# A gated mix of a state-space convolution and a squared-ReLU layer, backward pass: the S4 loop written out as a software pipeline, and FFT intermediates on other DMA queues

## The chip, the cores and the metric

The kernel runs on one core of a Trainium2 chip. The core has a matrix engine (TensorE, PE), a vector engine (VectorE, DVE), a scalar engine (ScalarE, ACT), a general engine (GpSimd, POOL) and SyncE (SP), which issues transfers; ACT and POOL issue transfers as well. Each engine works through its own queue of instructions in the order in which it was written. The metric is the device time of one execution in microseconds (us).

## The reference

The reference computes a mix of two branches and the gradients of all inputs. Cut to what matters:

```python
def A(u, A_re, A_im, B_re, B_im, C_re, C_im, log_dt, Dskip):   # S4 branch, D=448, N=256, L=2048
    dt = exp(log_dt)[:, None]
    logdA = dt * (A_re + 1j * A_im)
    P = exp(logdA[:, :, None] * arange(L))
    K = einsum("dn,dnl,dn->dl", C, P, dt * B).real
    return causal_conv_by_fft(u, K) + u * Dskip
def B(x, w1, b1, w2, b2):                                       # F=1792
    return relu(x @ w1 + b1) ** 2 @ w2 + b2
def f(u, ..., gate_w):
    g = sigmoid((u * gate_w).sum(-1, keepdims=True))
    return g * A(u, ...) + (1 - g) * B(u, ...)
out, vjp = jax.vjp(f, ...)
return out, *vjp(grad_out)
```

## The kernel before, in words

The S4 branch needs, for each of the 448 channels, the sequence K of 2048 values (a sum over 256 modes of powers of a complex number) and, backward, the sums of dK against the same powers. A power with exponent l is split into two factors, of 32 and of 64 steps, so that two small tables stand for it.

**S4 loop (lines 557 to 679).** It goes over NCH = 14 chunks of 32 channels (4 groups g of 8). For each chunk `build` makes table X (in the tile XW) in 4 doublings and table Y in 5, each doubling three operations on DVE (L549 and L550 multiply, L555 adds) with n = 4 to 32 for X and n = 2 to 32 for Y; ACT writes the first entries (L567 to L580). `kgen` multiplies the tables into K's values (128 matmuls at L593, out by one ACT cast, L597). `tables_t` transposes X on PE (L613) and copies it out on ACT (L614). `load_yt` transposes one group of Y by a DMA from SP (L622). `back` multiplies the transposed Y with dK (PE, L642; the second half of its weights is a scaled copy of dK by ACT, L631), casts the result (ACT, L645), forms two products per group on DVE (L654, 8 for a chunk), and sums these on PE (L663) into one PSUM tile kept over two chunks. X, Y and the PSUM tile for `kgen` and the transposes have one buffer each; the transposed Y (YT) and the products have three, the cast result two.

dK comes from an FFT correlation of `grad_out` and u ahead of the loop: `fwd1` (L173, evacuated alternately on ACT at L159 and DVE at L161), written to memory (gd, L178), read back (`load_s1`, L182), `fwd2` (L192), complex products (L202 to L207), `inv1` (L220), written and read back again (hd, L224 and L229), in four quarters q. After the loop K goes the same way.

**What sets the order.** A framework takes the program text in the order written, schedules it by its own costs, and writes each engine's queue; waits between engines are semaphores. Work of the dense branch fills in: its forward pass (L502, L513) lies beside the correlation, its backward pass beside the S4 loop, as loads by DMA transposes (L774, L810; weights at L786, L802) and matmuls (stage 1 at L779, stage 2 at L821). `K.dma()` gives its transfers to SP and ACT by turns.

In the loop one chunk follows the other:

```python
    for c in range(NCH):
        build(c)
        kgen(c)
        XTs = tables_t(c)
        back(c, XTs, [load_yt(g) for g in range(3)])
```

## Time and profile before

| what | value |
|---|---|
| time, median of 3 runs | 1341.72 us (1338.66 to 1354.12) |
| profiled execution, its own time | 1360.1 us |
| span of that execution in the trace | 1358.3 us |
| PE busy | 726.1 us (53%) |
| DVE busy | 865.4 us (64%) |
| ACT busy | 558.4 us (41%) |
| POOL busy | 136.7 us (10%) |
| mean granted clock of PE | 0.716 |

No engine is busy throughout. The page cuts the span into 40 slices; DVE's busy share by slice is `3465788666094673280857759659568573199994` in tenths, and the share of the 16 DMA engines `9988664758977979969576640440431429754886`. Read together with the lines that run, the stretches are: loads (0 to 60 us), `fwd1` of u and `grad_out` (60 to 100), the dense forward pass (100 to 240), the rest of the correlation and the first table build (240 to 328), the S4 loop with the dense backward pass beside its first part (328 to 1139), K's FFT (1139 to 1200), and the end (1200 to 1358). A row of a timeline gives start, duration, engine, line, operation and tiles, and in brackets the idle time of the engine just before and what ended it.

### The profile page before, as it was taken

Reading aid. Unit: us, or ns where it says so; the run is one execution under the profiler, and the core shown is the slowest. Engines: PE = TensorE matmul, PEld = TensorE weight load, DVE = VectorE, ACT = ScalarE, POOL = GpSimd, SP = SyncE. Lnnn points to the kernel's source line nnn. Section 1 sums busy time; section 2 is a strip of 40 time slices with the busy share of each in tenths; the row PEclk is TensorE's granted clock in tenths of the full one; section 3 lists DMA queues with packets and bytes.
Section 4 is the critical chain, followed back from the end, with each engine's and each line's share of the span. In section 5 each row is a group of like instructions: output and inputs, shape, how many; then the busy total and the mean of one; then the engine's idle time right before and its main releaser. Section 6 shows DMA issues by size and latency. Waiting matters only on the chain. (4 is left out here: it accounts for less than half of the span.)

```text
span 1358.3 us, 17800 instructions
## 1 busy us (share of the span) xinstructions
PE 726.1 (53%) x7088; PEld 323.8 (24%) x7088; DVE 865.4 (64%) x1102; ACT 558.4 (41%) x865; POOL 136.7 (10%) x244
## 2 busy tenths in 40 slices
PE   0456999432297793466987541431513405334467
PEld 0111222111144352223443221221312303111112
DVE  3465788666094673280857759659568573199994
ACT  1256998443265352322563442533423503323302
POOL 1001331000011211121212001001001001000000
PEclk9976999765598997677998655656555656555559
DMA  9988664758977979969576640440431429754886
GB/s 201 210 182 287 214 212 178 263 173 192 185 142 161 199 160 147 145 111 122 158 176 157 127 70 21 76 67 21 79 53 34 67 20 231 221 160 153 243 187 133
DMA packets 300012, 201.74 MB, mean 149 GB/s; under 512 B 235685, under 2 KB 281769, under 8 KB 299033
## 3 DMA queue, kind: packets, MB, share of 16 engines
q1 hardware_dynamic: 252280, 96.03, 37.4%
q0 software_dynamic: 17952, 65.85, 16.5%
q10 hardware_dynamic: 29696, 38.72, 11.3%
q8 instruction: 55, 0.90, 0.3%
q14 instruction: 29, 0.23, 0.1%
HBM read 78.23 MB, written 67.44 MB: 107 GB/s over the span
## 5 line engine op out<-in xcount | busy, mean ns | idle before, releaser
L654 DVE TENSOR_TENSOR P<-R 128x2048 bf16<-128x2048 bf16 x112 | 133.9, 1223 | 307.4 <-ACT R L645 296.2
L645 ACT CAST R<-psF 128x1024 bf16<-128x1024 f32 x112 | 115.2, 1051 | 43.1 <-PE psF L642 34.2
L593 PE MATMUL psX<-Y,X 128*32 128x64 bf16 x1792 | 24.8, 223 | 200.0 <-DVE Y L555 198.2
L642 PE MATMUL psF<-R,K 64*32 64x256 bf16 x896 | 56.2, 396 | 133.2 <-DMA R<-Y 91.0
L159 ACT CAST st<-psF 128x896 bf16<-128x896 f32 x69 | 60.8, 909 | 111.2 <-PE psF L220 56.1
L663 PE MATMUL psS<-P,cb_sel 128*32 128x256 bf16 x896 | 91.2, 321 | 19.5 <-DVE P L654 19.3
L614 ACT COPY R<-psX 128x1024 bf16<-128x1024 bf16 x56 | 56.9, 1015 | 58.3 <-PE psX L613 58.2
L555 DVE TENSOR_TENSOR Y<-Y,F 128x256 bf16<-128x256 bf16 (+4 forms) x70 | 70.5, 1007 | 2.4
L593 PEld LDWEIGHTS <-X 128*32 128x32 bf16 x1792 | 22.9, 113 | 204.8 <-DVE Y L555 162.1
L549 DVE TENSOR_TENSOR Y<-Y,F 128x256 bf16<-128x256 bf16 (+4 forms) x70 | 70.4, 1006 | 1.9
L550 DVE TENSOR_TENSOR F<-Y,F 128x256 bf16<-128x256 bf16 (+4 forms) x70 | 69.7, 995 | 0.4
L549 DVE TENSOR_TENSOR X<-X,F 128x512 bf16<-128x512 bf16 (+3 forms) x56 | 64.8, 1158 | 1.9 <-ACT F L567 0.5
L550 DVE TENSOR_TENSOR F<-X,F 128x512 bf16<-128x512 bf16 (+3 forms) x56 | 64.5, 1151 | 1.9 <-ACT F L568 1.9
L555 DVE TENSOR_TENSOR X<-X,F 128x512 bf16<-128x512 bf16 (+3 forms) x56 | 64.8, 1156 | 1.4
L663 PEld LDWEIGHTS <-cb_sel 128*32 128x32 bf16 x896 | 52.4, 109 | 54.4 <-issue 45.0
L642 PEld LDWEIGHTS <-K 64*32 64x32 bf16 x896 | 24.9, 155 | 157.6 <-issue 64.6
L161 DVE CAST st<-psF 128x896 bf16<-128x896 f32 x27 | 29.4, 1089 | 51.0 <-DMA gd<-st 26.4
L821 PE MATMUL psN<-D,S 128*128 128x448 bf16 x224 | 51.3, 377 | 16.5 <-DMA S<-dhT_d 16.5
L821 PEld LDWEIGHTS <-S 128*128 128x128 bf16 x448 | 42.5, 102 | 70.0 <-DMA S<-dhT_d 18.7
L613 PE MATMUL psX<-ident,X 128*128 128x128 bf16 x448 | 52.7, 291 | 11.7 <-ACT R L614 10.7
L220 PE MATMUL psF<-P,cb_MI 64*128 64x448 bf16 x128 | 28.8, 560 | 56.1 <-DVE P L204 25.1
L642 PE MATMUL psF<-R,S 64*32 64x256 bf16 x896 | 57.5, 365 | 0.5 <-ACT S L631 0.5
(202 smaller groups left out, 1520.8 us busy)
## 6 DMA issues: line engine op xcount, KB each, us to landing
hT_d<-R POOLq DMA_DIRECT2D x14, 512.0 KB, 3.8
sp<-K POOLq DMA_DIRECT2D x8, 896.0 KB, 5.1
dhT_d<-R POOLq DMA_DIRECT2D x14, 512.0 KB, 3.6
S<-hT_d POOLq DMA_DIRECT2D x8, 896.0 KB, 8.0
S<-dhT_d POOLq DMA_DIRECT2D x8, 896.0 KB, 6.8
rec_d<-rec POOLq DMA_DIRECT2D x14, 416.0 KB, 4.0
rec<-rec_d POOLq DMA_DIRECT2D x14, 416.0 KB, 3.5
gd<-st ACTq DMA_DIRECT2D x24, 224.0 KB, 3.7
```

The costliest lines, as they stand in the source:

```text
L159: nc.scalar.copy(dst, src)
L549: V.tensor_tensor(out=hi, in0=lo, in1=bcast_dims(pr, [0, (None, n // 2), 1]), op=ALU.mult)
L550: V.tensor_tensor(out=Vv.rearrange("p (x a q) -> p x a q", x=rows, q=2), in0=lo, in1=bcast_dims(pi, [0, (None, n // 2), 1]), op=ALU.mult)
L555: V.tensor_tensor(out=T4[:, :, :, n:2 * n], in0=T4[:, :, :, n:2 * n], in1=V4, op=ALU.add)
L593: T_.matmul(ps[32 * g:32 * g + 32, i * 64:(i + 1) * 64], lhsT=XW[:, 1 - t, w, :, 1], rhs=Y[:, w, t, :], start=(k == 0), stop=(k == 3), til ...
L613: T_.transpose(pt[:, 2 * t + i2, h * P:(h + 1) * P], XW[:, t, w:w + 4, :, 0].rearrange("p w a -> p (w a)"), ident[:])
L614: S.copy(XT[:, gg].rearrange("p t i n -> p (t i n)"), pt[:].rearrange("p a n -> p (a n)"))
L642: T_.matmul(psz[32 * ii:32 * ii + 32, t, 256 * s:256 * s + 256], lhsT=(DK[64 * t:64 * t + 64, :, d] if s == 0 else DKB[64 * t:64 * t + 64, ...
L645: S.copy(zb[:, :, :, i2, :], psz[:].rearrange("p t (s n) -> p t s n", s=2))
L654: V.tensor_tensor(out=pr.rearrange("p t s i n -> p t s (i n)"), in0=zv, in1=(xb if r == 0 else rev_dim(xb, 1)), op=ALU.mult)
L663: T_.matmul(sps[32 * gr:32 * gr + 32, r, :], lhsT=sel[:, k, off:off + 32], rhs=Q[r][:, t, s, i2, :], start=(g < 2 and cc == 0 and i2 == 0 ...
L821: T_.matmul(ps[:, 0:D], lhsT=blk[w][:, j, P * tt:P * tt + P], rhs=(w2n if w == 0 else w1T)[:, j, :], start=(w == 1 and j == 0), stop=(j == ...
```

## The change

Two things change. First, the transfers of FFT intermediates: all gd and hd writes go to ACT's queue (they went to SP and ACT by turns), all reads of them to SP's, and the write of the spectra (L454) goes from POOL's queue to ACT's. The turns that other loads take with `K.dma()` shift with it. Second, `build` is split into `build_x` and `build_y`, `tables_t` into its two pairs of groups, `back` into two halves, and the loop is written so that the tables of chunk c are built among the products of chunk c−1. The number of buffers does not change. Behind the loop every line number is higher than before by 3 to 13: L593 is now L596, L597 L600, L614 L616, L622 L624, L642 L645, L645 L648, L654 L657, L663 L666, L774 L787, L802 L815, L821 L834.

```diff
@@ fwd1, load_s1
-                    self.dma().dma_start(dst, st[g2 * 64:(g2 + 1) * 64])
+                    nc.scalar.dma_start(dst, st[g2 * 64:(g2 + 1) * 64])
...
-        self.dma().dma_start(s1.rearrange("p a d -> p (a d)"), src)
+        self.nc.sync.dma_start(s1.rearrange("p a d -> p (a d)"), src)
@@ inv1, load_hs
-            self.dma().dma_start(dst, st[:])
+            nc.scalar.dma_start(dst, st[:])
...
-            self.dma().dma_start(hs[64 * hp:64 * hp + 64].rearrange("p g x d -> p g (x d)"), src)
+            self.nc.sync.dma_start(hs[64 * hp:64 * hp + 64].rearrange("p g x d -> p g (x d)"), src)
@@ spectra
-            nc.gpsimd.dma_start(dst, sp.rearrange("p a r d -> p (a r d)"))
+            nc.scalar.dma_start(dst, sp.rearrange("p a r d -> p (a r d)"))
@@ the loop
-    for c in range(NCH):
-        build(c)
-        kgen(c)
-        XTs = tables_t(c)
-        back(c, XTs, [load_yt(g) for g in range(3)])
+    XTs, YTs = {}, {}
+    for c in range(NCH + 1):
+        if c < NCH:
+            build_x(c)
+            XTs[c] = tables_t(c, 0)
+        if c > 0:
+            back(c - 1, XTs[c - 1], YTs[c - 1], 0)
+        if c < NCH:
+            XTs[c] += tables_t(c, 1)
+            build_y(c)
+            kgen(c)
+        if c > 0:
+            back(c - 1, XTs[c - 1], YTs[c - 1], 1)
+        if c < NCH:
+            YTs[c] = [load_yt(g) for g in range(3)]
```

How the queues stand, at three places. DVE, the end of one chunk's table build and the start of the next chunk's, before (X and Y are the tables, R holds the cast results and transposed tables, P the products, F scratch):

```order
L549 TENSOR_TENSOR Y_271_1934<-Y_271_1934,F_273_1936 128x128x32
L550 TENSOR_TENSOR F_273_1936<-Y_271_1934,F_273_1936 128x4096
L555 TENSOR_TENSOR Y_271_1934<-Y_271_1934,F_273_1936 128x128x32
L654 TENSOR_TENSOR P_276_1939<-R_275_1938 128x2048 x7
L549 TENSOR_TENSOR X_272_1935<-X_272_1935,F_273_1936 128x128x4
L654 TENSOR_TENSOR P_276_1939<-R_275_1938 128x2048
L550 TENSOR_TENSOR F_273_1936<-X_272_1935,F_273_1936 128x512
```

DVE in the change, the same place, from the start of a chunk's build of X:

```order
L549 TENSOR_TENSOR X_272_1935<-X_272_1935,F_273_1936 128x128x4
L550 TENSOR_TENSOR F_273_1936<-X_272_1935,F_273_1936 128x512
L555 TENSOR_TENSOR X_272_1935<-X_272_1935,F_273_1936 128x128x4
L549 TENSOR_TENSOR X_272_1935<-X_272_1935,F_273_1936 128x128x8
L550 TENSOR_TENSOR F_273_1936<-X_272_1935,F_273_1936 128x1024
L657 TENSOR_TENSOR P_276_1939<-R_275_1938 128x2048
L555 TENSOR_TENSOR X_272_1935<-X_272_1935,F_273_1936 128x128x8
L657 TENSOR_TENSOR P_276_1939<-R_275_1938 128x2048
L549 TENSOR_TENSOR X_272_1935<-X_272_1935,F_273_1936 128x128x16
L550 TENSOR_TENSOR F_273_1936<-X_272_1935,F_273_1936 128x2048
L657 TENSOR_TENSOR P_276_1939<-R_275_1938 128x2048
L555 TENSOR_TENSOR X_272_1935<-X_272_1935,F_273_1936 128x128x16
```

Before, the eight products of a chunk stand behind both its tables, seven of them together. Now products of the chunk before (L657) stand one by one inside the doublings, from X's n = 8 on; a chunk's last eight operations of Y (n = 8 and above) have none between them.

ACT, from the cast of K's values on, before:

```order
L597 CAST st_6075<-psX_5946 128x512
L569 COPY X_272_1935<-rec_6349 128x128
L572 COPY X_272_1935<-rec_6349 128x128
L614 COPY R_275_1938<-psX_6078 128x1024
L645 CAST R_275_1938<-psF_6122 128x4x256
L614 COPY R_275_1938<-psX_6088 128x1024
L645 CAST R_275_1938<-psF_6140 128x4x256
L614 COPY R_275_1938<-psX_6098 128x1024
```

ACT in the change, from the same cast on (L672 is the copy of the sums, once in two chunks):

```order
L600 CAST st_6442<-psX_6313 128x512
L672 COPY st_6553<-psS_5727 128x512
L570 COPY X_272_1935<-rec_6566 128x128
L573 COPY X_272_1935<-rec_6566 128x128
L648 CAST R_275_1938<-psF_6610 128x4x256
L648 CAST R_275_1938<-psF_6628 128x4x256
L648 CAST R_275_1938<-psF_6665 128x4x256
```

The copies that seed the next table X (L569 and L572 before, L570 and L573 now) stand directly behind the cast in both. Before, copies of transposed tables (L614) alternate with the casts of `back` (L645); now four casts (L648) follow each other, and the copies of tables (L616) stand later.

SP, the transposes of the loop's second chunk among loads of the dense backward pass (L774 and L787 for stage 1), before:

```order
L774 DMA_TRANSPOSE S_274_1937<-hT_d 128x16x128
L622 DMA_TRANSPOSE R_275_1938<-Y_271_1934 128x16x128 x3
L786 DMA_TRANSPOSE S_274_1937<-S_274_1937 128x4x128
L622 DMA_TRANSPOSE R_275_1938<-Y_271_1934 128x16x128
L774 DMA_TRANSPOSE S_274_1937<-dhT_d 128x16x128
```

SP in the change, the transposes of the first and the second chunk:

```order
L624 DMA_TRANSPOSE R_275_1938<-Y_271_1934 128x16x128 x2
L799 DMA_TRANSPOSE S_274_1937<-S_274_1937 128x4x128
L787 DMA_TRANSPOSE S_274_1937<-hT_d 128x16x128
L624 DMA_TRANSPOSE R_275_1938<-Y_271_1934 128x16x128
L787 DMA_TRANSPOSE S_274_1937<-dhT_d 128x16x128 x3
L624 DMA_TRANSPOSE R_275_1938<-Y_271_1934 128x16x128 x4
L799 DMA_TRANSPOSE S_274_1937<-S_274_1937 128x4x128
```

Before, one chunk's four transposes of Y stood three and one with a weight load between; eleven loads stood ahead of the second chunk's. Now five loads in all stand between the first chunk's third transpose and the second chunk's first, and the second chunk's four stand together.

## Rows read from the trace of the kernel before

**Rows 1.** Windows: length, busy PE, PEld, DVE, ACT, POOL (count), PEclk, DMA share, GB/s.

```profile
100.00:240.00 140.00, 126.09 (x476) 35.04 (x475) 105.44 (x172) 116.73 (x249) 33.74 (x57) 0.91 0.66 225
328.40:608.00 279.60, 174.01 (x1937) 91.19 (x1937) 149.04 (x140) 109.20 (x172) 38.61 (x62) 0.77 0.90 158
608.00:793.20 185.20, 129.36 (x1457) 66.55 (x1455) 113.05 (x106) 77.69 (x112) 27.11 (x39) 0.84 0.66 137
793.20:1113.90 320.70, 110.03 (x2112) 69.44 (x2112) 225.03 (x210) 119.58 (x157) 17.83 (x35) 0.56 0.30 52
```

**Rows 2.** Timeline, ACT: the cast of K's values, chunks 0, 1, 8 and 13.

```profile
330.42 0.58 ACT L597 CAST st<-psX 128x512 bf16<-128x512 f32 x1 [2.99 <-PE psX L593]
411.81 0.59 ACT L597 CAST st<-psX 128x512 bf16<-128x512 f32 x1 [2.65 <-PE psX L593]
849.16 0.58 ACT L597 CAST st<-psX 128x512 bf16<-128x512 f32 x1 [3.01 <-PE psX L593]
1115.94 0.59 ACT L597 CAST st<-psX 128x512 bf16<-128x512 f32 x1 [33.00 <-PE psX L593]
```

**Rows 3.** Timeline, all engines, around the start of chunk 7's products.

```profile
790.89 2.29 DVE L555 TENSOR_TENSOR Y<-Y,F 128x4096 bf16<-128x4096 bf16 x1
793.33 1.93 PE L593 MATMUL psX<-Y,X 128*32 128x64 bf16 x128 [21.95 <-DVE Y L555]
796.08 1.07 ACT L572 COPY X<-rec 128x128 bf16<-128x128 bf16 x1
799.04 0.48 PE L642 MATMUL psF<-R,K 64*32 64x256 bf16 x8 [3.78 <-DMA R<-Y]
801.63 1.02 ACT L645 CAST R<-psF 128x1024 bf16<-128x1024 f32 x1
804.80 2.36 DVE L654 TENSOR_TENSOR P<-R 128x2048 bf16<-128x2048 bf16 x2 [11.62 <-ACT R L645]
817.36 0.42 DVE L549 TENSOR_TENSOR X<-X,F 128x512 bf16<-128x512 bf16 x1
```

**Rows 4.** Page, costliest groups: the products.

```profile
L654 DVE TENSOR_TENSOR P<-R 128x2048 bf16<-128x2048 bf16 x112 | 133.9, 1223 | 307.4 <-ACT R L645 296.2
```

**Rows 5.** Lines by shape, DVE, 793.2 to 1113.9 us (six chunks).

```profile
L654 DVE TENSOR_TENSOR P<-R 128x2048 bf16<-128x2048 bf16 x48 | 57.7, 1223 | 92.3 <-ACT R L645 88.9 <-PE psS L663 3.3
L549 DVE TENSOR_TENSOR X<-X,F 128x1024 bf16<-128x1024 bf16 x6 | 4.2, 693 | 0.2
```

**Rows 6.** Timeline, SP, DVE and PE, around chunk 3's products.

```profile
522.84 28.67 SPq L802 DMA_TRANSPOSE D<-in_B_w_dram  x2
551.61 9.01 SPq L622 DMA_TRANSPOSE R<-Y  x3
562.02 2.36 DVE L654 TENSOR_TENSOR P<-R 128x2048 bf16<-128x2048 bf16 x2 [41.73 <-ACT R L645]
608.62 13.80 SPq L622 DMA_TRANSPOSE R<-Y  x3
626.77 4.73 PE L821 MATMUL psN<-D,S 128*128 128x448 bf16 x14 [7.53 <-DMA S<-dhT_d]
633.72 1.40 PE L593 MATMUL psX<-Y,X 128*32 128x64 bf16 x128
```

**Rows 7.** Timeline, PE: the first matmuls of the first chunk's products.

```profile
362.53 0.69 PE L642 MATMUL psF<-R,K 64*32 64x256 bf16 x16 [30.43 <-DMA K<-dk_d]
```

**Rows 8.** Timeline, PE: `inv1` of two successive quarters of the correlation.

```profile
249.92 0.93 PE L220 MATMUL psF<-D,cb_MI 64*128 64x448 bf16 x4 [5.24 <-DVE D L204]
267.63 0.93 PE L220 MATMUL psF<-D,cb_MI 64*128 64x448 bf16 x4 [4.25 <-DVE D L204]
```

**Rows 9.** Windows: one quarter of the correlation; columns as in rows 1.

```profile
249.92:267.63 17.71, 8.71 (x48) 3.31 (x49) 10.73 (x11) 7.05 (x8) 1.06 (x2) 0.69 0.74 277
```

**Rows 10.** Line L178 (gd writes): issue time (least, median, greatest ns), and who waited (us, times).

```profile
L178 ACTq DMA_DIRECT2D gd<-st x24: 582/608/760, 31.1 to 1172.3; - x24
  ACT st L159: 26.7, 12
```

More of the change, by code (lines that the diff above doesn't have):

```diff
@@ L559, with build_x @@
     xi = yi = zi = pi_ = ki = 0
-    sps = None
-    def build(c):
+    sps = rec = None
+    def build_x(c):
+        nonlocal rec
         rec = K.t("rec", [P, NF, W2])
@@ L598, in kgen, with tables_t @@
         G_.dma_start(bass.AP(tensor=k_d, offset=c * P * 512, ap=[[512, P], [1, 512]]), kst[:])
-    def tables_t(c):
+    def tables_t(c, gp):
         nonlocal xi
         XTs = []
-        for gp in range(2):
-            XT = RB[:, xi % 3].rearrange("p (g t i n) -> p g t i n", g=2, t=2, i=2)
-            xi += 1
-            for gg in range(2):
-                g = 2 * gp + gg
-                pt = K.ps("X", [P, 4, 256], bf16)
-                for t in range(2):
-                    for i2 in range(2):
-                        for h in range(2):
-                            w = g * 16 + h * 8 + 4 * i2
-                            T_.transpose(pt[:, 2 * t + i2, h * P:(h + 1) * P], XW[:, t, w:w + 4, :, 0].rearrange("p w a -> p (w a)"), ident[:])
-                S.copy(XT[:, gg].rearrange("p t i n -> p (t i n)"), pt[:].rearrange("p a n -> p (a n)"))
-                XTs.append(XT[:, gg])
+        XT = RB[:, xi % 3].rearrange("p (g t i n) -> p g t i n", g=2, t=2, i=2)
+        xi += 1
+        for gg in range(2):
+            g = 2 * gp + gg
+            pt = K.ps("X", [P, 4, 256], bf16)
+            for t in range(2):
+                for i2 in range(2):
+                    for h in range(2):
+                        w = g * 16 + h * 8 + 4 * i2
+                        T_.transpose(pt[:, 2 * t + i2, h * P:(h + 1) * P], XW[:, t, w:w + 4, :, 0].rearrange("p w a -> p (w a)"), ident[:])
+            S.copy(XT[:, gg].rearrange("p t i n -> p (t i n)"), pt[:].rearrange("p a n -> p (a n)"))
+            XTs.append(XT[:, gg])
         return XTs
@@ L623, in load_yt, with back @@
         return YT
-    def back(c, XTs, YTs):
+    def back(c, XTs, YTs, half):
         nonlocal zi, pi_, sps
         cc = c % GC
-        if cc == 0:
+        if cc == 0 and half == 0:
             sps = K.ps("S", [P, 2, 256])
         DKB = DKBs[:, c % 2]
-        S.activation(DKB, DK[:].rearrange("p a (g x) -> p a g x", g=NG)[:, :, :, CW * c:CW * (c + 1)], ACT.Copy, scale=brow[:, 0:1])
-        for g in range(NG):
+        if half == 0:
+            S.activation(DKB, DK[:].rearrange("p a (g x) -> p a g x", g=NG)[:, :, :, CW * c:CW * (c + 1)], ACT.Copy, scale=brow[:, 0:1])
+        for g in (2 * half, 2 * half + 1):
             zb = RB[:, 6 + zi % 2].rearrange("p (t s i n) -> p t s i n", t=2, s=2, i=2)
@@ L665, in back @@
                                       tile_position=(0, 32 * gr), skip_group_check=True)
-        if cc == GC - 1:
+        if cc == GC - 1 and half == 1:
             gi = c // GC
```

1 line of the change is left out of this document (added).

## The prediction, made before the change was run

> **What bounds the kernel now.** I read the windows by stretch first [rows 1]: the reader is to see in each which engine is busy nearly throughout. From 100 to 240 us it is PE (126.09 of 140). In the first part of the S4 loop (328.4 to 608) no engine is, but the transfer engines are at 0.90. From 608 to 793.2 nothing is (DVE 113.05 of 185.2, transfers 0.66). In six chunks without dense work beside them (793.2 to 1113.9, clean chunks below) DVE has 225.03 of 320.7 us, 37.5 for a chunk, and transfers are at 0.30.
>
> Next the cast of K's values, which comes once in a chunk, as a clock [rows 2]: chunk 0 to 1 takes 81.4 us, chunk 0 to 8 518.7, chunk 8 to 13 266.8, which is 53.4 for a clean chunk against DVE's 37.5. So 15.9 us in each is idle DVE. The timeline says where [rows 3]: table Y ends at 793.18, its transposes start, and the first product starts at 804.80 after 11.62 us, released by the cast of `back`; the next X starts at 817.36, after the products. Over the loop the products wait 307.4 us, 296.2 of them for that cast [rows 4]; in the six clean chunks 92.3, or 15.4 each [rows 5]. DVE's chain there is Y, transpose, matmul, cast, products, next X, next Y, one after another. The chain runs through a stall of DVE that other DVE work could fill.
>
> **The change, part by part.**
>
> **Clean chunks.** The work on every engine is the same; what moves is the products, out of the place behind Y into the next X and Y. After Y's end, T, the next X can't start at once: it has one buffer, which K's matmuls read, and ACT seeds it behind the cast. Those stand in the old order: matmuls at 793.33, the last seed copy from 796.08 for 1.07 [rows 3], so X starts at T + 4.0. Ahead of the first product stand three operations of 0.42 (n = 4, rows 3) and two of 0.69 (n = 8, [rows 5]), 2.65 together, to T + 6.65. The first product needs a transposed Y, landed at T + 5.9 (799.04 against 793.18), 16 matmuls, about 1.0 as two of the groups of 8 take 0.48 each, and two casts of 1.02 [rows 3]: T + 8.9. DVE waits 2.3 there. Later casts have doublings of DVE between them; I count 0.5 for small gaps, and 0.7 for the copy of the sums every second chunk and the sums that products wait for (3.3 in six chunks, rows 5). The chunk is 4.0 + 2.3 + 0.5 + 0.7 + 37.5 = 45.0. The ends: 44.3 without the 0.7; 47.0 if the first product still starts 11.62 after T (idle 11.62 − 2.65 = 9.0, plus 0.5). I take 45.0, since the copies of X's tables that stood between the first casts now stand behind them. Five intervals (8 to 13): 266.8 − 225 = **−42** (−45 to −32). The last chunk's products have no table build to lie in, as before: 0.
>
> **Chunks beside dense work.** Here transfers set the pace. Their work from 328.4 to 793.2 is 0.90 × 279.6 + 0.66 × 185.2 = 374 us at full share [rows 1]. A clean chunk's own is 0.30 × 320.7 / 6 = 16.0, seven chunks 112; 262 is left for the dense work and dK. Chunk 0 to 8 then needs 262 + 8 × 16 = 390. At the 0.90 that the first part shows this is 433 us; at the mean share of both, 374 / 464.8 = 0.80, it is 487. Eight chunks of 45 are 360, so DVE isn't the limit. The two ends are rows of the same stretch; the new order spreads the loads more evenly over the chunks than the old (11 ahead of the second chunk's transposes, now 5), but keeps the weight loads ahead of a chunk's transposes: at 522.84 they hold SP for 28.67 us, Y's transposes start at 551.61, and DVE has idled 41.73 when its product starts at 562.02 [rows 6]. That stall is met one chunk later in the new order, so it stays. I take the middle, 460: **−59** (−86 to −32). The first chunk's wait for dK, 30.43 on PE [rows 7], lies in this sum: only X's first two doublings and a bit of the second chunk can be done before it.
>
> **The queues.** In the new order one more quarter of the correlation is inverted inside the dense forward pass. A quarter takes 17.71 us from one to the next [rows 8], 8.71 of it PE work [rows 9]; PE is what bounds the stretch it moves into, so 17.7 − 8.7 = −9. Against that, both halves of each gd write are now issued by ACT, one behind the other, 0.608 each [rows 10], ahead of ACT's next evacuation. The evacuation waits for these writes already (26.7 us in 12 times). Sixteen tiles ahead of the loop and eight behind it: 9.7 and 4.9 if all is on the path, 0 if the second buffer hides it; I take half, +5 and +2. The eight spectra writes moved from POOL to ACT, some 5 us of issue at the same price, lie beside PE in a stretch with ACT at 116.73 of 140 [rows 1]: 0, or +5 without that cover. Of the 24 hd writes half come over to ACT, 7 us at that price, each behind its own evacuation: 0, or +7 if all delay the next. Sum −4 and +2; the ends are −9 (no issue on the path) and +27 (all of them, and the quarter gains nothing).
>
> By the Trainium skill, page "DMA: Bandwidth & Descriptors", section "Issuing engines are not separate DMA queues", the issuing engine changes nothing but sequencer time, all transfers running on the same 16 engines. If so the −9 would be 0 and the total 9 us higher; the trace here shows no run with the other queues, and SP's 28.67-us weight load ahead of Y's transposes shows that what stands behind what in one queue does cost time.
>
> **Sum.** −42 − 59 − 4 + 2 = −103. The profiled execution took 1360.1 us, 18.4 (1.4%) above the median of 1341.7; taken off the median this gives **1238** (1257 for an execution like the profiled one). This case runs from −45 − 86 − 9 = −140 (1202) to −32 − 32 + 27 = −37 (1305).
>
> **Rivals.**
>
> *Transfers don't limit (faster).* If loads find gaps, every chunk takes 45 and only dK's wait of 30 stays: 8 × 45 + 30 = 390, −129 − 42 − 2 = −173, 1169. For it: the share falls to 0.66 in the second part. Against: 0.90 in the first.
>
> *The dense stretch gives nothing.* A late transpose of Y now holds up not only products but the table build, since a product stands in the middle of it and DVE takes its queue in order; before, the build was done by then. And the dense matmuls stay ahead of K's: Y's end had long come and transposes had started (608.62) when K's matmuls ran at 633.72, behind a dense group that itself waited 7.53 for its load [rows 6]. The next X waits for K's matmuls. If this eats the gain, −42 − 2 = −44, 1298.
>
> *Slower: these stalls add up.* If all eight intervals beside dense work become as long as the first, 81.4 [rows 2], they make 651, +132; with −44 from the rest it is +88, 1430. It decides from a mean interval of (518.7 + 44) / 8 = 70.3 us on, where it was 64.8. Against it: the dense work is unchanged, its 262 us of transfers leave room in 519, and the wait for dK, which makes the first interval long, comes once.
>
> By the Trainium skill, page "TensorE: Matmul & The Clock Gate", section "Architectural detail: the array is 16× 32×32, not 1× 128×128", PE's queue pulls only weight loads forward, and ACT and DVE are strict first-in-first-out. The trace agrees: the ready matmuls of K stood behind the 7.53-us wait. This is the rule that speaks against the change, and what it would make of the time are the last two cases.
>
> *The change doesn't do what it says.* K's matmuls, X's seeds and Y's transposes all start at Y's end as before. If the wait only moves into the doublings, the clean chunk stays 53.4 and the time about 1340. Against it: work of 2.65 us and more stands between, and X is free 4.0 us after Y's end.
>
> **How the numbers follow.** The forecast has 0.62, the unlimited case 0.08, no gain beside dense work 0.18, slower 0.06, no effect 0.06. The forecast and the third case fill 1202 to 1305; with some room below for the spread of the runs the range is 1195 to 1305, which leaves out the 0.20 of the others. 1% is 13 us, about what can be told from no change: faster 0.62 + 0.08 + 0.18 = 0.88, same 0.06, slower 0.06.
>
> **What would show it.** In clean chunks the casts of K's values some 45 us apart, 4.0 us from Y's end to the next X, and a wait of 2 to 3 us, not 11.6, before a chunk's first product. Chunk 0 to 8 in about 460 us, with transfers at 0.85 or so. The first cast about 4 us earlier than 330.42. I am wrong if clean chunks stay above 48 us, which fails the main step; if DVE waits for casts inside the doublings beside dense work for more than some 10 us a chunk, which is the third case; or if the stretch from chunk 0 to 8 passes 563 us, which is the fourth.

## The result, and the profile after

The changed kernel takes 1249.14 us (median of 4 runs, 1246.45 to 1258.18), the kernel before 1344.81 (1338.66 to 1354.12): the ratio is 0.9295, with a 95% interval of 0.922 to 0.9369. It is 95.7 us faster; 103 were forecast, and 1238 us. The profiled executions stand apart by more, 113.7 us of span (1358.3 to 1244.6), since that of before was 15.3 above its median and that of after (1246.45) is 2.7 below. Which part of the kernel holds those 15.3 us isn't known.

Rows of engines and lines, from the page of the kernel after. First what answers to the table of before, then the products [rows 4] and the first operation of X's doublings (busy, mean ns | idle time before it, what ended it):

```profile
PE 719.5 (58%) x7088; PEld 315.2 (25%) x7088; DVE 855.9 (69%) x1102; ACT 559.8 (45%) x865; POOL 131.8 (11%) x236
L657 DVE TENSOR_TENSOR P<-R 128x2048 bf16<-128x2048 bf16 x112 | 136.7, 1223 | 141.7 <-ACT R L648 107.8
L549 DVE TENSOR_TENSOR X<-X,F 128x512 bf16<-128x512 bf16 (+3 forms) x56 | 64.8, 1157 | 58.1 <-ACT X L573 57.0
```

The work is the same (DVE 865.4 us before, 855.9 now); the products' idle time fell from 307.4 us to 141.7, and 58.1 us, nearly all new, stand before X's first doubling.

The cast of K's values as a clock, after (timeline of ACT; answers to [rows 2]; chunks 0, 5, 8 and 13):

```profile
340.00 0.58 ACT L600 CAST st<-psX 128x512 bf16<-128x512 f32 x1 [2.12 <-PE psX L596]
638.27 0.58 ACT L600 CAST st<-psX 128x512 bf16<-128x512 f32 x1 [2.65 <-PE psX L596]
792.82 0.58 ACT L600 CAST st<-psX 128x512 bf16<-128x512 f32 x1 [2.55 <-PE psX L596]
1008.37 0.58 ACT L600 CAST st<-psX 128x512 bf16<-128x512 f32 x1 [11.44 <-PE psX L596]
```

The table takes the time apart by this clock (of the profiled executions, so a piece of before can be too long by part of those 15.3 us). The time from one chunk's cast to the next is called an interval below.

| piece | before | after | difference | forecast |
|---|---|---|---|---|
| start to the first cast | 330.4 | 340.0 | +9.6 | −4 |
| chunk 0 to 8, beside dense work | 518.7 | 452.8 | −65.9 | −59 |
| chunk 8 to 13, clean | 266.8 | 215.5 | −51.2 | −42 |
| last cast to the end | 242.4 | 236.2 | −6.1 | +2 |
| sum of the spans | 1358.3 | 1244.6 | −113.7 | −103 |

A clean chunk takes 43.1 us, 53.4 before. Its start, after (timeline, all engines; answers to [rows 3]): the end of Y, K's matmuls, X's first operation, the first matmuls of the products, their first two casts, and the first product.

```profile
788.45 2.29 DVE L555 TENSOR_TENSOR Y<-Y,F 128x4096 bf16<-128x4096 bf16 x1
790.79 1.96 PE L596 MATMUL psX<-Y,X 128*32 128x64 bf16 x128 [7.90 <-DVE Y L555]
795.15 0.43 DVE L549 TENSOR_TENSOR X<-X,F 128x512 bf16<-128x512 bf16 x1 [4.41 <-ACT X L573]
797.12 0.47 PE L645 MATMUL psF<-R,K 64*32 64x256 bf16 x8 [4.37 <-DMA R<-Y]
797.87 1.93 ACT L648 CAST R<-psF 128x1024 bf16<-128x1024 f32 x2 [2.75 <-PE psF L645]
799.83 1.23 DVE L657 TENSOR_TENSOR P<-R 128x2048 bf16<-128x2048 bf16 x1 [2.12 <-ACT R L648]
```

Y ends at 790.74. X starts 4.4 us later (3.9 in chunks without the copy of the sums), where 4.0 were forecast. The first product starts 9.1 us after Y's end (8.2 in the next chunk), where 8.9 were forecast, after a wait of 2.12, forecast 2.3; before, the wait was 11.62. The pipeline does in the clean part what it was said to do.

Windows of the kernel after, with the columns of [rows 1], cut at casts: chunk 0, chunks 1 to 3, chunk 4, chunks 5 to 7, and the five clean chunks:

```profile
340.00:412.00 72.00, 34.78 (x390) 16.37 (x393) 37.34 (x35) 32.58 (x50) 3.64 (x7) 0.62 0.81 172
412.00:562.00 150.00, 124.83 (x1486) 64.07 (x1475) 109.98 (x105) 76.95 (x118) 24.43 (x41) 0.88 0.87 170
562.00:638.00 76.00, 39.99 (x473) 20.44 (x474) 36.61 (x35) 25.31 (x38) 16.35 (x23) 0.73 0.88 153
638.00:793.00 155.00, 114.22 (x1418) 57.99 (x1407) 110.14 (x105) 74.66 (x107) 23.81 (x35) 0.86 0.70 151
793.00:1008.00 215.00, 88.30 (x1772) 57.36 (x1774) 183.25 (x175) 98.29 (x128) 16.71 (x33) 0.61 0.38 69
```

Transfers are at 0.81 to 0.88 until chunk 5 and at 0.70 from there to chunk 8, some 0.80 over the stretch, where 0.85 or so was forecast. That share turned out not to be the reason for the pace there.

### The profile page after: what moved, and what is told of

It reads as the page before. It is cut to its first block, busy times and chain, and to the rows that moved or that the text cites. A ratio compares the mean times of both kernels' runs of the same rounds, so it can differ in the third digit from the quotient of the medians.

```text
span 1244.6 us, 17711 instructions
## 1 busy us (share of the span) xinstructions
PE 719.5 (58%) x7088; PEld 315.2 (25%) x7088; DVE 855.9 (69%) x1102; ACT 559.8 (45%) x865; POOL 131.8 (11%) x236
## 5 line engine op out<-in xcount | busy, mean ns | idle before, releaser
L657 DVE TENSOR_TENSOR P<-R 128x2048 bf16<-128x2048 bf16 x112 | 136.7, 1223 | 141.7 <-ACT R L648 107.8
L648 ACT CAST R<-psF 128x1024 bf16<-128x1024 f32 x112 | 112.4, 1047 | 107.9 <-PE psF L645 101.6
L645 PE MATMUL psF<-R,K 64*32 64x256 bf16 x896 | 53.3, 414 | 159.3 <-DMA R<-Y 129.7
L549 DVE TENSOR_TENSOR X<-X,F 128x512 bf16<-128x512 bf16 (+3 forms) x56 | 64.8, 1157 | 58.1 <-ACT X L573 57.0
L666 PE MATMUL psS<-P,cb_sel 128*32 128x256 bf16 x896 | 89.5, 321 | 4.9 <-DVE P L657 3.9
L616 ACT COPY R<-psX 128x1024 bf16<-128x1024 bf16 x56 | 58.0, 1035 | 50.8 <-PE psX L615 48.0
L645 PEld LDWEIGHTS <-K 64*32 64x32 bf16 x896 | 26.8, 154 | 191.5 <-issue 113.6
L615 PE MATMUL psX<-ident,X 128*128 128x128 bf16 x448 | 42.3, 250 | 38.3 <-DVE X L555 30.9
L596 PE MATMUL psX<-Y,X 128*32 128x64 bf16 x1792 | 24.0, 221 | 67.2 <-DVE Y L555 67.2
L666 PEld LDWEIGHTS <-cb_sel 128*32 128x32 bf16 x896 | 51.7, 109 | 42.3 <-issue 32.1
L792 PE MATMUL psN<-D,S 128*128 128x448 bf16 x224 | 55.7, 378 | 5.8 <-ACT D L775 4.8
L792 PE MATMUL psN<-U,S 128*128 128x449 bf16 x224 | 53.6, 378 | 2.6 <-DMA S<-dhT_d 2.6
L834 PE MATMUL psN<-U,S 128*128 128x448 bf16 x224 | 53.8, 376 | 0.0
```

What stands on the lines that cost most here:

```text
L549: V.tensor_tensor(out=hi, in0=lo, in1=bcast_dims(pr, [0, (None, n // 2), 1]), op=ALU.mult)
L615: T_.transpose(pt[:, 2 * t + i2, h * P:(h + 1) * P], XW[:, t, w:w + 4, :, 0].rearrange("p w a -> p (w a)"), ident[:])
L616: S.copy(XT[:, gg].rearrange("p t i n -> p (t i n)"), pt[:].rearrange("p a n -> p (a n)"))
L645: T_.matmul(psz[32 * ii:32 * ii + 32, t, 256 * s:256 * s + 256], lhsT=(DK[64 * t:64 * t + 64, :, d] if s == 0 else DKB[64 * t:64 * t + 64, ...
L648: S.copy(zb[:, :, :, i2, :], psz[:].rearrange("p t (s n) -> p t s n", s=2))
L657: V.tensor_tensor(out=pr.rearrange("p t s i n -> p t s (i n)"), in0=zv, in1=(xb if r == 0 else rev_dim(xb, 1)), op=ALU.mult)
```

## The experiments

Each kernel was run beside the kernel before; ratios are to that, and the changed kernel's own is 0.9295. The runs of before gave medians from 1344.8 to 1355.4 from set to set, so two kernels of different sets that lie within some 10 us are told apart by their profiles alone. The runs with the queue moves, the pipeline, the weight loads left out, and the products behind all of X are one set; those with the bias gradient as rows, half of the dense loads, the products behind the middle of X, and X's seeds on DVE a second; the other four a third; the changed kernel stands apart from all three. Lines are those of the changed kernel unless the kernel before is named.

### The queue moves alone

```diff
  (the kernel before, with only)
-                    self.dma().dma_start(dst, st[g2 * 64:(g2 + 1) * 64])
+                    nc.scalar.dma_start(dst, st[g2 * 64:(g2 + 1) * 64])
...
  (and the other four moves of the change; the loop as it was)
```

> The kernel before with the queue moves alone; the loop is as before. Theory A (the pipeline made the whole gain, the queue moves cost time ahead of the loop): the first cast of K's values comes at about 338 us against 330.4 before, the clean chunk stays at 53.4, and the time is 5 to 10 us above before. Theory B (the queue moves change nothing, only who issues): within 3 us of before. Theory C (part of the 95 us came from a freer SP queue beside the dense backward pass): chunk 0 to 8 falls from 518.7 to below 500 and the time is 15 us or more below before.

Measured: 1347.28 us, 0.9966 (0.9934 to 0.9998). In the profile the first cast comes at 341.9 (before: 330.4), chunk 0 to 8 takes 496.1 (518.7), a clean chunk 53.1, the rest 239.0 (242.4). Theory A is right on the start and on the clean chunks, and wrong on the sum, since 22.6 us came back beside dense work, which is the first half of theory C: the 113.4-us interval of before has no counterpart, another one of 88.7 stands a chunk earlier. In the medians it is next to nothing, as B said, so some of the 22.6 can be the 15.3 us by which the profile of before lies above its median. The first matmul that needs dK runs at 377.47, 15 us later than in the kernel before [rows 7].

### The pipeline alone

```diff
  (the changed kernel, with all five queue moves undone)
-                    nc.scalar.dma_start(dst, st[g2 * 64:(g2 + 1) * 64])
+                    self.dma().dma_start(dst, st[g2 * 64:(g2 + 1) * 64])
...
```

> The changed kernel with all queue moves undone, the pipelined loop alone. Theory A: the first cast comes at about 330 us instead of 340.0, chunk 0 to 8 takes about 453 and the clean chunk 43.1 as in the changed kernel; the time is 5 to 10 us below the changed kernel, about 1240. Theory B: the same time as the changed kernel, within 3 us. Theory C: chunk 0 to 8 is longer than 470 and the time 15 us or more above the changed kernel.

Measured: 1254.33 us, 0.9295 (0.924 to 0.9351): the same ratio as with the moves, which is theory B. So the pipeline makes the gain, and the moves add nothing that can be measured. The pieces differ, though. The timeline of DVE in this kernel, the end of the first Y and the next X:

```profile
327.11 2.29 DVE L555 TENSOR_TENSOR Y<-Y,F 128x4096 bf16<-128x4096 bf16 x1
364.04 0.43 DVE L549 TENSOR_TENSOR X<-X,F 128x512 bf16<-128x512 bf16 x1 [34.64 <-ACT X L573]
```

The first table is ready at 329.4 (after: 337.94), but the next X waits 34.64 us, because its seed copies stand on ACT behind the scaled copy of dK. The first matmul with dK runs at 360.42 instead of 373.99, and the clock reaches chunk 8 at 785.3 against 792.8. Behind the loop the old queues lose it again: 245.3 us from the last cast to the end against 236.2.

### Dense weight loads left out

```diff
-    for dt in range(DT):
-        z = DSZ[dt]
-        nc.sync.dma_start_transpose(out=w1T[:, :, dt * P:dt * P + z], in_=B_w1[dt * P:dt * P + z, :])
...
-                    T_.matmul(..., rhs=(w2n if w == 0 else w1T)[:, j, :],
+                    T_.matmul(..., rhs=w2n[:, j, :],
```

> The changed kernel without the four transposed loads of the dense branch's weights w1 that stand ahead of one chunk's transposes of Y; the last dense products use w2 in their place. Theory A (late transposes of Y, held up in SP's queue, stop the whole table build on DVE, since a product stands in its middle): the wait of 31.3 us in chunk 4 to 5 falls below 12 and that interval from 76.1 to about 53, the time by about 22 us. Theory B (the transfer engines set the pace of the stretch, whatever the order): the time falls by the loads' own share alone, under 10 us, and the wait turns up elsewhere in chunks 5 to 8. Theory C (PE's dense products ahead of K's matmuls set the pace): no change within 3 us.

Measured: 1248.79 us, 0.9254 (0.9218 to 0.929), within the noise of the changed kernel. The first product of the chunk that stalls, in this kernel (timeline, DVE):

```profile
592.77 1.23 DVE L657 TENSOR_TENSOR P<-R 128x2048 bf16<-128x2048 bf16 x1 [23.04 <-ACT R L648]
```

It still waits 23.04 us, and the interval is 69.2 instead of 76.1. Theory A is refuted in its size: 8 us of the wait go with the weight loads, which let the transposes of Y be issued 6.5 us earlier (562.29, not 568.77); the larger part stays, and the time with it, as theory B said. What is that part? The same place in the changed kernel, POOL's timeline, then two windows (columns as above), then the product:

```profile
562.56 1.09 POOL L804 DMA_DIRECT2D out_dram<-db  x1 [2.87 <-ACT db L798]
588.49 0.50 POOL L677 DMA_DIRECT2D s_d<-st  x1 [19.80 <-DMA out_dram<-db]
```
```profile
570.00:575.00 5.00, 0.00 (x0) 0.00 (x0) 0.00 (x0) 0.00 (x0) 0.00 (x0) 0.50 0.88 9
575.00:580.00 5.00, 0.00 (x0) 0.00 (x0) 0.00 (x0) 0.00 (x0) 0.00 (x0) 0.50 0.56 21
```
```profile
599.09 1.23 DVE L657 TENSOR_TENSOR P<-R 128x2048 bf16<-128x2048 bf16 x1 [31.32 <-ACT R L648]
```

At 562.56 POOL issues the gradient of the bias b1: 3.5 KB, an array of 128 partitions by 14 values whose neighbours in memory lie on different partitions, so by its access pattern it is 1792 single values of 2 bytes. POOL's next wait for it ends at 588.49. From 570 to 580 no engine computes, and the transfer engines, 0.88 and 0.56 busy, move 9 and 21 GB/s. A write of 3.5 KB is under way there, and everything behind it waits; the next run takes it away.

### The bias gradient as rows

```diff
-    G_.dma_start(out_11.rearrange("(t p) -> p t", p=P), db1[:])
+    pdb = K.ps(NT[ni % 2], [P, 4, 256], bf16)
+    ni += 1
+    T_.transpose(pdb[0:FT, 0, 0:P], db1[:], ident[:])
+    dbr = const.tile([FT, P], bf16, name="dbr")
+    S.copy(dbr[:], pdb[0:FT, 0, 0:P])
+    G_.dma_start(out_11.rearrange("(t p) -> t p", p=P), dbr[:])
```

> The changed kernel with the gradient of the bias b1 (3.5 KB, written before in pieces of 2 bytes) turned by PE first and written as 14 rows of 256 bytes; nothing else. Theory A (that write clogs the transfer engines: from 570 to 585 us they show 0.56 to 0.89 busy and move 9 to 130 GB/s while all compute engines stand still, and POOL waits 19.8 us for it): the wait of 31.3 us in chunk 4 to 5 falls below 12, the interval from 76.1 to about 53, the time by 18 to 25 us. Theory B (the large w2 load, 1568 KB and 29.4 us to landing, and the loads beside it make the stall): the wait stays above 20 and the time within 5 us.

Measured: 1233.42 us, 0.9108 (0.9048 to 0.9168), 16 us below the changed kernel, and the two intervals of the ratios don't meet. The same product, in this kernel:

```profile
583.39 1.23 DVE L657 TENSOR_TENSOR P<-R 128x2048 bf16<-128x2048 bf16 x1 [14.21 <-ACT R L648]
```

The wait falls from 31.32 to 14.21, the interval from 76.1 to 58.8. Theory A, with its size a little high. The load of w2 (1568 KB) that B named takes 29.4 us to land in the changed kernel and 12.6 here, so it was held up itself. The 14.21 us that are left lie behind it and behind the transposed loads of w1, after which Y's transposes are issued here (576.05); no run left w2 out. The edit also moves the write: it needs a transpose and a copy first and is issued at 575.70, behind the load of w2, where the old one stood ahead of it. Its shape and its place weren't tried apart.

### The bias gradient as rows, in the kernel before

The edit above, in the kernel before.

> The kernel before with the bias gradient written as 14 rows of 256 bytes. Theory A: there the write (at 573.4 us) comes after DVE's 41.73-us wait (to 562.0), which is the w1 loads', but it clogs the loads of the dense second stage after it, and K's matmuls at 633.7 stand behind the matmuls that wait for these; interval 3 to 4 falls from 113.4 by 15 to 30 us and the time by as much. Theory B: the write only hurts where DVE waits at that moment: interval and time within 6 us of before.

Measured: 1329.22 us, 0.986 (0.9767 to 0.9953), some 19 us by the ratio. Interval 3 to 4 falls from 113.4 to 84.4, as theory A said. In the kernel before, POOL's timeline and a window show the write (L791 there) and the low rate behind it, and in this kernel DVE's and PE's timelines show that the long wait of [rows 6] stays (41.73 before) while K's matmuls come at 605.14 instead of 633.72:

```profile
573.40 1.10 POOL L791 DMA_DIRECT2D out_dram<-db  x1
591.42 0.50 POOL L674 DMA_DIRECT2D s_d<-st  x1 [5.96 <-DMA out_dram<-db]
```
```profile
582.00:589.00 7.00, 7.00 (x37) 3.26 (x35) 6.86 (x6) 0.70 (x2) 3.00 (x6) 1.00 0.81 27
```
```profile
557.89 2.36 DVE L654 TENSOR_TENSOR P<-R 128x2048 bf16<-128x2048 bf16 x2 [37.31 <-ACT R L645]
```
```profile
605.14 1.40 PE L593 MATMUL psX<-Y,X 128*32 128x64 bf16 x128
```

So the worst interval of before had two causes, one after the other: a wait of some 40 us for transposes of Y behind large loads, and then the bias write (27 GB/s in that window), which made dense matmuls late, with K's matmuls behind them on PE. The prediction saw the first, and took the second for a load's.

### Half of the dense loads

```diff
-            hh = hn[:, (2 * j + w) % 4]
-            src = hT_d if w == 0 else dhT_d
-            nc.sync.dma_start_transpose(out=hh, in_=bass.AP(tensor=src, offset=j * P * L, ap=[[L, P], [1, L]]))
+            hh = hn[:, (2 * j) % 4]
+            if w == 0:
+                nc.sync.dma_start_transpose(out=hh, in_=bass.AP(tensor=hT_d, offset=j * P * L, ap=[[L, P], [1, L]]))
```

> The changed kernel with 14 of the 28 transposed loads of the dense backward pass's first stage left out (the second operand's tiles; the first operand's tile is used in their place, with the same matmuls). Theory A (transfers set the pace of the stretch beside dense work): 14 loads at some 4 us of all transfer engines each, as the transposes of Y of the same size take 16.0 for four, are 56 us; chunk 0 to 8 falls from 452.8 to between 385 and 410, the time by 40 to 65 us. Theory B (single stalls in the order of the queues set it, each behind something else than those loads): chunk 0 to 8 falls by less than 20. Theory C (PE's dense matmuls ahead of K's): no change within 5 us.

Half of the 28 loads of the first dense stage are gone; those of the second stage stay. Measured: 1239.58 us, 0.9159 (0.9102 to 0.9216). Chunk 0 to 8 is 445.7, 7.1 less, within theory B's 20. The three intervals in which most of these loads lie are 47.6, 51.1 and 47.7 (47.2, 52.6 and 49.9). The window of these three intervals, in this kernel:

```profile
408.00:555.00 147.00, 124.67 (x1459) 64.43 (x1458) 109.98 (x105) 77.72 (x121) 24.52 (x41) 0.88 0.73 139
```

The transfer share there is 0.73 instead of 0.87 and the pace is the same, so the share doesn't set it; PE is busy 124.67 of 147 us, DVE 109.98. Theory A, on which the prediction built its largest term, is refuted for these chunks.

### Half of the dense matmuls

```diff
-            for t in range(LT):
+            for t in range(LT // 2):
...
-                for j in range(FT):
+                for j in range(FT // 2):
```

> The changed kernel with half of the matmuls of the dense backward pass left out (8 of 16 terms in its first stage's sums, 7 of 14 in the second's), all of its loads kept. Since leaving out 14 loads took only 7 us off chunk 0 to 8, Theory A: in the six intervals there without the wait for dK or the stall of the bias write (47.2, 52.6, 49.9, 56.1, 49.3, 49.2 against 43.1 clean: 46 us together) the price is PE's: dense matmuls stand ahead of K's, of the products' and of the sums' matmuls in its queue. With half of them chunk 0 to 8 falls from 452.8 by 20 to 40 us. Theory B (loads and transposes on SP): the loads are the same, so it falls by less than 8.

Measured: 1276.93 us, 0.9463 (0.9359 to 0.9567): slower than the changed kernel, which neither theory said. Leaving work out let the framework pack the dense work into six chunks instead of eight, so the edit changed the order as well. The window of two of them:

```profile
412.00:539.00 127.00, 81.61 (x912) 38.95 (x912) 73.40 (x70) 57.73 (x96) 26.42 (x43) 0.79 1.00 201
```

Here transfers are at 1.00, intervals 61.3 and 64.2, and over the stretch PE's queue stands 44.6 us, in 8 times, behind dense matmuls that wait for their loads; 26.5 of this is one wait, behind the bias write. It is an experiment on another schedule and doesn't tell what sets the 47 to 53 us in the changed kernel. The two chunks of the window hold 21 of the first stage's loads, where the changed kernel has 22 in three (SP's timeline), and move 201 GB/s where it moves 170. That looks like transfers setting the pace, but no run took loads away from this schedule.

### The products behind all of X

```diff
-        if c > 0:
-            back(c - 1, XTs[c - 1], YTs[c - 1], 0)
+        if c > 0 and c < NCH:
+            with tc.issue_after(xl):      # xl: last operation of build_x(c)
+                back(c - 1, XTs[c - 1], YTs[c - 1], 0)
...
```

> The changed kernel with the products of the chunk before queued on DVE behind the whole of table X, not from its second doubling on. Theory A (the first product waits for the transposed Y and the casts, fixed at about 8.9 us after Y's end, and stands too early): the wait of about 2 us before the first product in clean chunks goes, the clean chunk falls from 43.1 to about 41.3; beside dense work up to 11 us of each late transpose is hidden, in all some 20 to 40 us; time 1205 to 1235. Theory B (what the build gains the products lose: casts and sums run into the next Y's end, the last products wait): the clean chunk stays at 43 and the time within 5 us of the changed kernel. Theory C (transfers set the pace beside dense work): only the clean chunks gain, about 10 us.

Measured: 1280.24 us, 0.9471 (0.9422 to 0.9521), slower than the changed kernel by 1.9% in the ratios; the last four clean chunks take 46 to 47. Neither theory has this: B comes nearer, with no gain, but said 43 and not slower, and the mechanism is another. DVE's timeline in this kernel:

```profile
914.10 0.40 DVE L549 TENSOR_TENSOR Y<-Y,F 128x256 bf16<-128x256 bf16 x1 [4.79 <-ACT Y L584]
922.40 3.49 DVE L658 TENSOR_TENSOR P<-R 128x2048 bf16<-128x2048 bf16 x3
```

The framework put Y's first operation inside X. It waits for its seeds, and these for the chunk's last transpose to leave Y free; 4.79 us there, and the products now follow without a wait. In the changed kernel that operation came late enough behind the products.

### The products behind the middle of X

```diff
  (as above, with xl the second operation of X's doubling n = 16, and)
-            build_y(c)
+            with tc.issue_after(yl):      # yl: last product of back(c - 1), half 0
+                build_y(c)
```

> The changed kernel with the first product queued behind the second operation of X's third doubling (n = 16), and table Y's operations behind the first four products, so that Y's first operation, which waits for the last transpose of the chunk before, doesn't stand inside X as it did when the products stood behind all of X. Theory A (the products stood too early, and the loss with the products behind X came from Y's first operation): the wait of 2 us before the first product goes, Y's first operation waits under 1 us, the clean chunk is 41 to 41.5 against 43.1, the time 10 to 30 us below the changed kernel. Theory B (later products lose at the chunk's end what they gain at its start): 43 or more, as the 46 to 47 with products behind X, time no lower.

Measured: 1241.01 us, 0.9175 (0.9109 to 0.9242), 8 us below the changed kernel in the medians, which alone doesn't tell the two apart; the last four clean chunks take 42.2 on the mean, 43.1 in the changed kernel. DVE's timeline in this kernel:

```profile
901.43 1.23 DVE L661 TENSOR_TENSOR P<-R 128x2048 bf16<-128x2048 bf16 x1 [1.05 <-ACT R L652]
920.79 0.43 DVE L549 TENSOR_TENSOR X<-X,F 128x512 bf16<-128x512 bf16 x1 [3.93 <-ACT X L574]
```

The first product of a clean chunk, which waited 0.66 to 2.62 us, doesn't wait any more, and neither does Y's first operation; a later product now waits about 1 us (the first row). Theory A, with half of its size in the chunk and less in the time: X's start, 3.9 to 4.4 us after Y's end, is untouched.

### X's seeds on DVE

```diff
-        S.copy(XW[:, :, :, 0, 1], rec[:, 22:24])
+        V.tensor_copy(XW[:, :, :, 0, 1], rec[:, 22:24])
...
-        S.copy(XW[:, :, :, 1, 1], rec[:, 24:26])
+        V.tensor_copy(XW[:, :, :, 1, 1], rec[:, 24:26])
```

> The changed kernel with the two copies that seed the next X moved from ACT, behind the cast, to DVE. X can then start about 2.5 us after Y's end instead of 4.0 to 4.4. Theory A (the first product, fixed by transposed Y, matmul and casts at 8.2 to 9.1 us after Y's end, stands early in X and bounds this part, so the time goes into its wait): the wait before the first product grows by what X's start gains less one 0.69-us operation more ahead of it, the clean chunk is 42.5 to 43.5 against 43.1 and the time within 8 us of the changed kernel. Theory B (X's start bounds the chunk): the clean chunk is 41.5 or less and the time 15 us or more lower.

Measured: 1262.42 us, 0.9329 (0.9252 to 0.9405), which by the ratio isn't told apart from the changed kernel; the span is 15.1 us longer. The last four clean chunks are 42.4 to 43.6, as A said (the time is more than the 8 us off that it allowed), and the timeline shows why:

```profile
888.75 2.29 DVE L555 TENSOR_TENSOR Y<-Y,F 128x4096 bf16<-128x4096 bf16 x1
893.13 0.46 DVE L570 COPY X<-rec 128x128 bf16<-128x128 bf16 x1 [2.08 <-PE psX L596]
900.02 1.23 DVE L657 TENSOR_TENSOR P<-R 128x2048 bf16<-128x2048 bf16 x1 [2.77 <-ACT R L648]
```

X's seeds (L570) start 2.1 us after Y's end, and the first product at 900.02 is 9.0 us after it as ever; only its wait grew, to 2.77. The loss comes from elsewhere: chunk 0 to 8 is 9.6 us longer and the interval after it 7.4. In the one with the bias write (83.9) a product now waits 31.62 us for a sum on PE, with that write issued at 581.62, just ahead. PE's timeline there shows what the sum stands behind, a dense matmul that waits for its weights:

```profile
610.98 0.53 PE L834 MATMUL psN<-D,S 128*128 128x448 bf16 x1 [28.83 <-DMA D<-in_B_w_dram]
```

### Two gains together, and the gd writes split again

> The changed kernel with both gains so far: the bias gradient written as rows, and the products behind the second operation of X's third doubling. If the two are independent (-16 and -8 us) the time is 1225; if the stall hid the other's gain, down to 1218; if one takes the other's place, 1233.

Measured: 1223.75 us, 0.9085 (0.9013 to 0.9157), 25 us below the changed kernel and the lowest median of the study. In the medians the two gains add; by the ratios this kernel isn't told apart from the one with the rows alone (0.9108), and it is the profile that shows both: chunk 0 to 8 takes 436.5 (438.6 with the rows alone, 449.0 with the products alone), a clean chunk 42.4 (43.4 and 42.4).

```diff
  (the same, with the gd writes of the first two transforms)
-                    nc.scalar.dma_start(dst, st[g2 * 64:(g2 + 1) * 64])
+                    (nc.sync if alt and g2 else nc.scalar).dma_start(dst, st[g2 * 64:(g2 + 1) * 64])
```

> As the run before it, and the gd writes of the two transforms ahead of the loop again one on ACT and one on SP, those behind the loop left on ACT. Theory A (ACT's issue of both halves, 1.25 us for a pair ahead of the next evacuation, makes the 9.6 us by which the first cast of K's values comes later): the first cast comes at 330 to 334 us instead of 340 and the time is 5 to 10 us lower. Theory B (dK's arrival sets when the loop can go on, as in the kernel with the pipeline alone, where the first table was ready 8.5 us earlier and the gain was lost in the wait): chunk 0 to 1 grows by what the first cast gains, the time is within 4 us. Theory C (other transfers' moves did it): first cast still at 338 or later.

Measured: 1231.31 us, 0.9157 (0.9051 to 0.9263), not told apart from the one before. The first cast comes at 347.4, later, not earlier: theory A is refuted, and it is C's outcome, that the two writes on one queue are not what delays the start. Which of the other moves does wasn't tried further.

## Why the prediction was right, and where not

**Clean chunks: right, mechanism and size.** Forecast 45.0, measured 43.1. X's start (4.0 forecast, 3.9 to 4.4), the first product (8.9; 7.6 to 9.1) and the wait (2.3; 0.66 to 2.62) are as worked out. What was mis-sized is DVE's work: 183.25 us in five chunks, 36.6 each, not the 37.5 of [rows 1]. The last section says where the rest went.

**Chunks beside dense work: the size met by luck, the reason wrong.** The step "here transfers set the pace" failed. It read a transfer share of 0.90 as a bound; half of the first stage's loads gone took the share from 0.87 to 0.73 in three chunks and their time from 150 to 146 us. The clock says what the stretch is made of. Eight clean chunks of 43.1 are 345. The first interval is 29 longer (72.5), dK's wait, as forecast. The interval with the bias write is 33 longer (76.1), 17 of it that write. The other six are 46 us longer together, where before they were only 4 longer than clean ones. In the dense chunks, then, the pipeline gave 3 us each instead of 10.

So the 65.9 us by which the stretch became shorter are 8.9 in the first interval, 19.7 in those six, and 37.3 in the one with the stall (113.4 to 76.1), of which the forecast had said that it stays. Before, K's matmuls ran 25 us after Y's transposes had been issued there (633.72, 608.62 [rows 6]); in the changed kernel they run 1.1 us after Y's end at 635.76 (timeline, PE):

```profile
636.84 1.40 PE L596 MATMUL psX<-Y,X 128*32 128x64 bf16 x128
```

How much of these 37 us is the pipeline's isn't shown: with the queue moves alone the longest interval behind the first is 88.7, with the pipeline alone 84.4, and in the kernel before with the bias gradient as rows 84.4.

DVE's waits over the stretch (340 to 792.8), in chunks 1 to 3 (412 to 562) and 5 to 7 (638 to 793) of it, and then in the five clean chunks (us in total, times, longest):

```profile
DVE P L657 <- ACT R L648: 88.8, 11, 31.3
DVE P L657 <- PE psS L666: 29.2, 10, 5.0
```
```profile
DVE P L657 <- ACT R L648: 14.0, 3, 6.5
DVE P L657 <- PE psS L666: 12.9, 4, 5.0
```
```profile
DVE P L657 <- ACT R L648: 14.8, 3, 10.1
DVE P L657 <- PE psS L666: 13.3, 5, 4.4
```
```profile
DVE P L657 <- ACT R L648: 8.9, 5, 2.6
DVE P L657 <- PE psS L666: 0.8, 4, 0.2
```

The rows account for the 46 us of the six chunks. Products wait 26.2 us there for sums on PE, and six clean chunks would have 1.0: 25 us. They wait 28.8 for casts, against 10.7: 18 us. The last 3 are waits for X's seeds. The first part goes with PE's load: it is busy 124.83 of 150 us in chunks 1 to 3, and the sums' matmuls stand in its queue behind dense ones. The second goes back to transposes of Y that come later than in clean chunks (PE idles 8.03, 7.01 and 11.48 us for them in three of the six, 2.9 to 4.4 in clean ones). With half of the first stage's loads gone these waits are 11.9 us in chunks 1 to 3 instead of 14.0, so transfers have a part in them; the rest isn't explained. The first part is the third rival's mechanism (a product in the middle of the build stops the build), at part of its price. In the six chunks this is read from the rows and from the order of the instructions; the experiment that was to show it changed the schedule, so it stays argued there. In one place a trace shows it, in the kernel with X's seeds on DVE: a dense matmul waits 28.83 us on PE, and a product 31.62 for a sum behind it. The Trainium skill's rule that was set against the change (page "TensorE: Matmul & The Clock Gate", section "Architectural detail: the array is 16× 32×32, not 1× 128×128": matmuls, ACT and DVE keep their order) bore on the right place.

**The stall at the weight loads: a part of the cause only.** The prediction said that it stays and is met a chunk later. The wait did, 31.3 instead of 41.7 us, but without the weight loads 23.0 of it are still there, and with the bias write as rows 14.2. In the kernel before, the write comes after the wait and lengthens the interval behind it; that the weight loads make the wait there wasn't tried. POOL's queue was not read at that place: 39.66 us of waiting there, and the write behind it, stand in the trace of before.

**The queues: wrong sign at the start.** "One more quarter lies inside the dense forward pass, −9" failed: the quarter did not move forward, dense matmuls moved behind it. The last of them starts at 261.85 us, before at 239.94, and the third quarter comes 12.6 us later than in [rows 8]. In the kernel after (timeline of PE):

```profile
280.24 0.93 PE L220 MATMUL psF<-D,cb_MI 64*128 64x448 bf16 x4 [4.25 <-DVE D L204]
261.85 1.14 PE L513 MATMUL psS<-X,R 128*128 128x512 bf16 x4
373.99 0.42 PE L645 MATMUL psF<-R,K 64*32 64x256 bf16 x1 [17.26 <-DMA K<-dk_d]
```

dK comes at 373.99, before at 362.53 [rows 7]. With the moves PE also runs its first transforms at the lower clock: from 50 to 140 us the granted clock is 0.50 (1.2 GHz) with PE busy 40.71 us, before 0.79 with 50.20, and 0.83 with the pipeline alone. It fell to 0.50 at about 50 us (PE busy 1.59 us from 45 to 50) and rose from 140 us on (9.82 of 10 busy). In the kernel before it is at 1.00 (2.4 GHz) from 50 to 80 us, though PE there is busy 1.42 us from 45 to 50 and not at all in the next five. What makes the two differ, and what share of the late start it is, isn't shown. A pair of gd writes holds ACT's issue about 1.25 us, as the forecast had it, but splitting them again brought nothing back. Behind the loop the moves gained about 9 us with the pipeline (245.3 with the old queues, 236.2 with the new) and 3 without it (242.4, 239.0), where a loss of 2 was forecast. The sum of the moves is near zero in both kernels, made of +11 to +15 us at dK, a gain beside dense work in one kernel, and −3 to −9 at the end. The Trainium skill's rule that the issuing engine changes only issue time (page "DMA: Bandwidth & Descriptors", section "Issuing engines are not separate DMA queues") agrees with that sum; the pieces show that a move also changes what stands behind what in a queue.

**The sum** of the profiled pieces came out within 11 us because a start 14 us worse than forecast met three pieces that were 7 to 9 us better; the medians are 7 us from the forecast gain. That is luck in part: the clean chunks are as worked out, and the other pieces came about otherwise than the forecast said.

## What to carry to other kernels

When one engine waits a fixed time in each turn for a chain through three others, and has independent work of the next turn, put that work into the wait: the gain can be read beforehand from the wait and from what can start, and in the clean chunks here the reading was within 2 us a chunk. Where other work shares the engines' in-order queues, count on a part of it only, and look for the part in the queue of the engine that the new order makes wait. A high transfer share says that transfers are busy, not that they set the pace; take loads away before believing it, and look at the bytes moved in the windows in which nothing computes.

## What the runs showed of the hardware

With a write of 3.5 KB under way, whose values of 2 bytes lie apart in memory, the transfer engines were 0.56 to 0.88 busy at 9 to 21 GB/s for 10 us and the whole kernel waited with them; as 14 rows, issued behind another load instead of ahead of it, it landed in 3.3 and 5.2 us, and one kernel was 16 us faster and the other, by its ratio, 19. The Trainium skill's page "DMA: Bandwidth & Descriptors", section "Rules for kernel authors", says that a non-contiguous last dimension makes one descriptor per element; what that does to transfers behind it is shown here by the windows.

An operation of DVE that reads what the one before it wrote starts later than an independent one. Before, the add starts 1.25 us after the multiply of 1.22 that feeds it; after, a product lies between them, and each starts 1.13 or 1.14 after the one ahead (DVE's timeline, kernel before, then after):

```profile
823.10 1.22 DVE L550 TENSOR_TENSOR F<-X,F 128x2048 bf16<-128x2048 bf16 x1
824.35 1.22 DVE L555 TENSOR_TENSOR X<-X,F 128x2048 bf16<-128x2048 bf16 x1
```
```profile
803.85 1.22 DVE L550 TENSOR_TENSOR F<-X,F 128x2048 bf16<-128x2048 bf16 x1
804.98 1.22 DVE L657 TENSOR_TENSOR P<-R 128x2048 bf16<-128x2048 bf16 x1
806.12 1.22 DVE L555 TENSOR_TENSOR X<-X,F 128x2048 bf16<-128x2048 bf16 x1
```

In a clean chunk eight such pairs now have an independent operation between them, seven times a product; at 0.12 us each that is about the 0.9 us by which DVE's work in a clean chunk came out below the forecast (an estimate from these rows).
